# A third tile of the first head block as float32 products, other groups for the layer norm's factors, and x ahead of the weights in the opening of an attention and mixer-MLP kernel

## The chip, the cores and the metric

One Trainium2 chip, one core. The core has five engines that run their own queues and meet at semaphores: TensorE (PE; its weight loads are listed as PEld), VectorE (DVE), ScalarE (ACT), GpSimd (POOL) and SyncE (SP), from whose queue this kernel issues its DMA transfers. The metric is the time of one execution on the device in microseconds (us); lower is better. A kernel is executed several times, and the median stands for it.

## The reference

x has 2048 tokens of 512 channels. A layer norm without parameters is applied twice over, once for both branches and once more inside the second. Branch one is sliding-window attention with 32 heads of 16 channels, where each token sees itself and seven earlier ones at a distance of two. Branch two is an MLP 512 → 1376 → 512 with a tanh GELU.

```python
def _A_ref(x, wqkv, wo):                 # H=32 heads, Dh=16, W=8, dil=2
    qkv = (x @ wqkv).reshape(B, S, 3, H, Dh)      # -> q, k, v: B, H, S, Dh
    idx = pos[:, None] - (jnp.arange(W) * dil)[None, :]
    kg, vg = k[:, :, idx_c], v[:, :, idx_c]
    logits = einsum("bhsd,bhswd->bhsw", q, kg) * Dh ** -0.5   # idx < 0 masked
    o = einsum("bhsw,bhswd->bhsd", softmax(logits), vg)
    return o.reshape(B, S, D) @ wo
def _B_ref(x, w1, b1, w2, b2):
    h = gelu(layernorm(x) @ w1 + b1)
    return h @ w2 + b2
xn = layernorm(A_x)
return A_x + _A_ref(xn, wqkv, wo) * silu(_B_ref(xn, w1, b1, w2, b2))
```

## The kernel before, in words

Tokens are split into even and odd ones (`c` = 0, 1), since the window's distance is two; each half has eight tiles of 128 tokens by 512 channels, numbered 0 to 7. The heads come in four blocks of eight (`hb`). A unit is one half with one head block: its q, k, v columns (384) for eight tiles, then the attention of these heads on DVE and POOL. The MLP's two layers (`mlp1`, `mlp2`) run on TensorE between the units, so that DVE has time for the attention.

Products are made from f16 numbers in three passes: each operand is split into a high part (rounded to f16) and a low part (what is left), and high by high, low by high and high by low are summed. One tile's product with one head block is therefore 12 matmuls of 128x128 by 128x384. The weights are first scaled by a power of two that comes from their sum of squares (`scale_q`, L597 on ACT with `s` as its sum; L513 the sum over partitions on TensorE; L524 to L542 the exponent arithmetic on DVE, which yields `qsc`, `hsc`, `zsc`, `osc`). Then the high part is made on ACT (L619, L565) or DVE (L563), the low part on DVE (L626, L569) or, where a table says 'pool', by two POOL operations (L553 scales, L554 subtracts).

A planner records every operation with what it reads and writes, and issues them in the order of a table of operation numbers, `ORDER`; each engine works through its own part of that order. Which engine makes which part stands in tables at the top: `HI_ENG`, `W1ENG` (high parts), `QLO0`, `W1LO`, `W2LO` (low parts), `EV0`, `EV1` (which engine moves a finished product from its bank to SBUF). Buffers come from rings: `prod` (three of 128x2048, which also hold staged x and weights in the opening), `f`, and in PSUM `ps` (three banks), `pl` and `z0` to `z3` (one each). `U_93` and `U_94` are the two large SBUF buffers of the units' q, k, v; in the opening U_94 holds the transposed x and staged weights.

The opening belongs to the even half. Loads stand in SP's queue in the order of `LOADS`. Each tile of x (L1233) gets its statistics on DVE (L659, L660), then, for a group of tiles at once (`GROUPS`), `pb` on DVE (L714, L716) and the factor `rb` by a power on POOL (L718); `y` = normalised x is made on POOL (L748), ACT (L744) or DVE (L751), by tile. Tiles 0 to 3 are transposed on TensorE (L766: four transposes into a bank `z`), the high part is taken by ACT or DVE (L770, L772), the low part by DVE (L773). Tiles 4 to 7 get their f16 parts first (L756, L757) and are transposed by DMA (L758). The second norm's factor `cT` is made for a batch of tiles (`BATCHES`, L727 to L731) and folded into the scale with which a product leaves its bank (`cs`).

Those transposes and parts take time in which TensorE would have nothing to do. So for two tiles, 6 and 7 (`FP`), the product with the first head block is made directly in float32, from a transposed copy of x that the kernel loads ready-made (`A_xt`, L1258). `center(i)` takes the mean off: the sum over the four channel groups by DVE (L685) and one float32 matmul with a constant (L691), or the whole mean by four float32 matmuls (L682), as `MEANBY` says, then a subtraction in place on DVE (L693). `direct(i)` then makes four float32 matmuls 128x384 with the staged, unscaled weights (L700) into `pl` or a bank `z`. In the profile a float32 matmul shows as two rows. Later head blocks and the MLP use tiles 6 and 7 by the usual way.

TensorE's clock is kept up in the first microseconds by dummy matmuls (`WAKE`, L1305). After the opening come the units' matmuls (L864), evictions (L878 on DVE, L882 on ACT) and, from about 34 us, `mlp1` (L1143; its high part by ACT in L1156 and L1159, its low part by DVE in L1161) and `mlp2` (L1186, with the remainder in L1174 and L1177). The attention's multiplications and sums are L930, L933, L983 and L988 on DVE and L999 and L1010 on POOL. The output product is L1056 and L1088.

Of the kernel before, what the change touches and what calls it, by code (L numbers as in the profile page):

```python
# [10 lines left out]
BF16 = mybir.dt.bfloat16  # L11
# [7 lines left out]
P = 128  # L19
# [5 lines left out]
NI = 8  # L25
# [7 lines left out]
LASTP = 256  # L33
# [11 lines left out]
FP = (6, 7)  # L45
XC = (6, 7)
BYDMA = (4, 5, 6, 7)
TRZ = (3, 3, 0, 2, 0, 1, 1, 0)
PTR = (0.5487, 0.3388, 0.0342, 0.6565, 0.7826, 0.1978, 0.0549, 0.9)
GROUPS = ((0,), (1, 2), (3, 4, 5), (6, 7))  # L50
BATCHES = ((0, 1, 2, 3, 4, 5), (6, 7))
LOADS = (('t', 6), ('q', 0), ('q', 2), ('x', 2), ('x', 0), ('q', 4), ('t', 7), ('x', 5), ('x', 1), ('x', 3), ('x', 4), ('q', 6), ('w', 0), ('w', 2), ('x', 7), ('c', 2), ('s', 1), ('c', 0), ('w', 3), ('x', 6), ('w', 1), ('c', 1), ('b', 0), ('s', 0))
# [16 lines left out]
W2LATE = 6  # L69

# [309 lines left out]

# [1146 lines left out]
```

## Time and profile before

| what | value |
|---|---|
| median of 3 runs | 412.66 us (412.56 to 412.87) |
| span of the profiled execution | 411.0 us; its own time is not on the page |
| PE busy | 402.8 us (98%), 2030 matmul rows |
| DVE busy | 381.6 us (93%) |
| ACT busy | 224.9 us (55%) |
| POOL busy | 132.7 us (32%) |

The page and the answers of the trace share one manner of writing. `ps<-wq,yT` is an operation that reads buffers wq and yT and writes ps; `128x384 f32<-128x512 f32` are the shapes and types out and in; `x8` counts instructions of the same kind that follow each other; times are microseconds from the span's start. `<-DVE U L693` names what released an instruction after a wait: DVE's write of U in line 693. L numbers are lines of the kernel.

### The profile page before, as it was taken

What the parts mean: (1) busy time and instruction counts of PE and PEld (TensorE: products, weight loads), DVE (VectorE), ACT (ScalarE), POOL (GpSimd) and SP (SyncE); (2) the same over time, 40 slices, a digit from 0 to 9 for tenths busy, and PEclk for the clock granted to TensorE, in tenths of its full rate; (3) what the DMA queues carried; (4) which work ended last, traced back from release to release, by engine and by line L of the source; (5) the groups of instructions that cost most, each with busy time, mean ns of one, the idle gap of its engine ahead of it and who ended that gap; (6) DMA issues with size and microseconds to landing.
All of it is one profiled execution on the core that took longest, in us unless ns stands there. A gap on an engine that the chain in (4) does not pass through costs nothing.

```text
span 411.0 us, 5490 instructions
## 1 busy us (share of the span) xinstructions
PE 402.8 (98%) x2030; PEld 198.7 (48%) x2030; DVE 381.6 (93%) x386; ACT 224.9 (55%) x372; POOL 132.7 (32%) x141
## 2 busy tenths in 40 slices
PE   7899999999999999999999999999999999999996
PEld 4565544444444455445544554444445544444443
DVE  4899999999999999999889999899999989989985
ACT  3899987983989736633564164214523177236310
POOL 2843000053562425143424243233322505250012
PEclk9999999999999999999999999999999999999999
DMA  8957538251018372911251009610344452004984
GB/s 288 395 104 227 177 90 214 92 179 27 1 30 189 85 130 77 150 49 27 51 141 27 0 2 213 209 50 22 107 122 120 107 135 60 0 1 116 285 214 162
DMA packets 52627, 48.04 MB, mean 117 GB/s; under 512 B 37066, under 2 KB 37510, under 8 KB 52088
## 3 DMA queue, kind: packets, MB, share of 16 engines
q1 hardware_dynamic: 52600, 47.69, 42.8%
q8 instruction: 16, 0.26, 0.3%
q14 instruction: 11, 0.09, 0.1%
HBM read 24.40 MB, written 7.34 MB: 77 GB/s over the span
## 4 chain that ended last, share of the span: by engine, by line
PE 90%; DVE 3%; ACT 3%; DMA 1%; POOL 1%; issue 0%; SPq 0%; POOLq 0%; ACTq 0%; DVEq 0%
PE ps L864 27%; PE z L1186 25%; PE ps L1143 25%; PE ps L1056 5%; PE z L1088 2%; PE ps L1088 2%; PE z L1174 2%; DMA prod<-in_A_x_dram 1%; DVE bn L659 1%; ACT w L565 1%; ACT w L504 1%; PE pl L1088 1%; PE z L1177 1%; PE pl L864 1%; POOL prod L748 1%; DVE yT L773 0%
## 5 line engine op out<-in xcount | busy, mean ns | idle before, releaser
L864 PE MATMUL ps<-wq,yT 128*128 128x384 f16 (+1 forms) x708 | 128.9, 337 | 0.2
L1186 PE MATMUL z<-w,h 128*128 128x512 f16 x480 | 111.4, 379 | 0.0
L1143 PE MATMUL ps<-yT,w 128*128 128x512 f16 x480 | 109.0, 379 | 0.0
L864 PEld LDWEIGHTS <-yT 128*128 128x128 f16 x744 | 72.2, 98 | 59.1 <-issue 1.3
L930 DVE TENSOR_TENSOR prod<-U 128x2048 f32<-128x2048 f32 x32 | 73.8, 2312 | 4.1 <-ACT U L882 3.0
L1143 PEld LDWEIGHTS <-w 128*128 128x128 f16 x480 | 46.8, 98 | 55.6 <-issue 0.5
L933 DVE TENSOR_REDUCE L<-prod 128x128 f32<-128x2048 f32 x32 | 73.0, 2282 | 0.5
L1186 PEld LDWEIGHTS <-h 128*128 128x128 f16 x480 | 46.5, 98 | 54.6 <-issue 0.7
L999 POOL TENSOR_TENSOR prod<-prod,prod 128x1024 f32<-128x1024 f32 x14 | 41.3, 2968 | 81.3 <-DVE prod L988 81.3
L882 ACT ACTIVATE U<-ps,cs 128x384 f32<-128x384 f32 x54 | 30.1, 575 | 62.9 <-PE ps L864 62.7
L988 DVE TENSOR_TENSOR prod<-pl,U 128x2048 f32<-128x2048 f32 x28 | 63.5, 2283 | 0.3
L1156 ACT ACTIVATE ps<-ps,b1T,hsc 128x512 f32<-128x512 f32 x40 | 29.8, 747 | 37.0 <-PE ps L1143 36.8
L1159 ACT ACTIVATE h<-ps,hsc 128x512 f16<-128x512 f32 x40 | 27.4, 684 | 20.6 <-PE z L1186 19.7
L1009 POOL COPY gate<-prod 1x1 f32<-1x1 f32 x21 | 4.6, 219 | 102.2 <-DVE prod L930 102.2
L1010 POOL TENSOR_TENSOR prod<-prod 128x1024 f32<-128x1024 f32 x14 | 32.9, 2348 | 0.0
L1161 DVE SCALAR_TENSOR_TENSOR h<-ps,hsc,h 128x512 f16<-128x512 f32 x40 | 29.5, 744 | 3.2 <-ACT h L1159 3.2
L1056 PE MATMUL ps<-wo,oT 128*128 128x512 f16 x96 | 21.5, 379 | 0.0
L983 DVE TENSOR_TENSOR prod<-prod,prod 128x2048 f32<-128x2048 f32 x9 | 20.6, 2288 | 0.2
L971 ACT ACTIVATE o<-prod,osc 128x1024 f16<-128x1024 f32 (+1 forms) x9 | 9.5, 1051 | 18.0 <-DVE prod L983 9.9
L1010 POOL TENSOR_TENSOR prod<-prod,prod 128x1024 f32<-128x1024 f32 x7 | 16.4, 2347 | 0.0
L1088 PEld LDWEIGHTS <-oT 128*128 128x128 f16 x108 | 10.5, 98 | 10.4 <-issue 0.2
L1056 PEld LDWEIGHTS <-oT 128*128 128x128 f16 x96 | 9.4, 98 | 11.1
(201 smaller groups left out, 393.6 us busy)
## 6 DMA issues: line engine op xcount, KB each, us to landing
f<-in_A_x_dram SPq DMA_DIRECT2D x31, 256.0 KB, 3.1
U<-U SPq DMA_DIRECT2D x16, 392.0 KB, 6.7
gd<-f SPq DMA_DIRECT2D x12, 256.0 KB, 2.7
prod<-in_A_x_dram SPq DMA_DIRECT2D x8, 256.0 KB, 5.7
oT<-in_B_w_dram SPq DMA_DIRECT2D x2, 1024.0 KB
yT<-in_B_w_dram SPq DMA_DIRECT2D x2, 1024.0 KB
f<-gd SPq DMA_DIRECT2D x8, 256.0 KB, 5.4
out_dram<-f SPq DMA_DIRECT2D x8, 256.0 KB
```

The source lines that it names most:

```text
L864: nc.tensor.matmul(b.t[:, 0:wide], y[:, s, k, o:o + P], wq[hb][:, t, k], start=(n == 0), stop=(n == 11))
L882: act(384, lambda i=i, b=b: nc.scalar.activation(U3[:, i:i + 31:15, :], b.t[:, 0:384].rearrange("p (t e) -> p t e", t=3), AF.Identity, sca ...
L930: dve(2048, lambda p2=p2, g=g: nc.vector.tensor_tensor(p2(), q, slots(Ut, KH, 2 * g), op=ALU.mult), qk + [("kh", ub, 0), ("kh", ub, 1), (" ...
L933: dve(2048, lambda pr=pr, g=g: nc.vector.tensor_reduce(L3()[:, 2 * g:2 * g + 2], pr.t.rearrange("p (r f d) -> p r f d", r=2, d=DH), AX.X, ...
L988: dve(2048, lambda: nc.vector.tensor_tensor(pr.t.rearrange("p (r f d) -> p r f d", r=2, d=DH), A3()[:, 2 * g:2 * g + 2].rearrange("p r (f ...
L999: pool(2.4, lambda n=n: nc.gpsimd.tensor_tensor(acc.t[:, n:n + 1024], acc.t[:, n:n + 1024], p1.t[:, n:n + 1024], op=ALU.add), [acc, p1], [ ...
L1010: nc.gpsimd.tensor_tensor(x.t[:, 0:1024], x.t[:, 0:1024], y(), op=ALU.add)
L1056: nc.tensor.matmul(b.t, oT[:, hb, i // 4, s, i % 4], wo[:, t, hb], start=(hb == 0 and n == 0), stop=(hb == last and n == 2))
L1088: nc.tensor.matmul(b.t[:, cols], oT[:, hb, i // 4, s, i % 4], wo[:, t, hb, cols], start=(start and hb == 0 and n == 0), stop=(stop and hb ...
L1143: nc.tensor.matmul(b.t[0:M], w1[:, s, f * 512 + k * M:f * 512 + (k + 1) * M], yT[ch][:, t, k], start=(n == 0), stop=(n == 11))
L1156: act(512, lambda: nc.scalar.activation(b.t[0:M], b.t[0:M], AF.Gelu_apprx_tanh, bias=b1T[0:M, f:f + 1], scale=hsc[0:M, 1:2]), [b, ("b1T",) ...
L1186: nc.tensor.matmul(z.t, hl[s][:, t * P:(t + 1) * P], w2[:, w, f], start=(f == 0 and n == 0), stop=False)
```

## The change

It does the following.

- Tile 5 joins tiles 6 and 7: its product with the first head block is made in float32 into a third bank (z2). Its sum is taken by DVE. Its transposed x is a third load of that kind, and takes a place of its own in U_94.
- The groups of the layer norm's factor are (0), (1, 2), (3, 4), (5, 6, 7) instead of (0), (1, 2), (3, 4, 5), (6, 7), and the batches of the second factor (0 to 4), (5, 6, 7).
- SP's queue begins with x of tiles 0, 2 and 1, and the first half of the weights comes after x of tile 6 and two transposed tiles.
- 28 dummy matmuls instead of 19.
- Other engines for some parts: three of w1's high parts, and half of the second head block's, move from ACT to DVE; low parts of w1 move from DVE to POOL, and of w2 index 3 instead of index 5 is POOL's; of the evictions some change between ACT and DVE.
- A new table `ORDER`, and planner prices for POOL's operations. Several new options (`SUBS`, `ST_ENG`, `YLO`, `SECS`, `QH0`) stand at values that leave the code as it was; `LASTC` gives the same two parts as `LASTP` did.

```diff
-FP = (6, 7)
-XC = (6, 7)
+FP = (6, 7, 5)
+XC = (6, 7, 5)
-TRZ = (3, 3, 0, 2, 0, 1, 1, 0)
+TRZ = (3, 3, 3, 0, 0, 2, 0, 0)
-GROUPS = ((0,), (1, 2), (3, 4, 5), (6, 7))
-BATCHES = ((0, 1, 2, 3, 4, 5), (6, 7))
+GROUPS = ((0,), (1, 2), (3, 4), (5, 6, 7))
+BATCHES = ((0, 1, 2, 3, 4), (5, 6, 7))
-HI_ENG = ('act', 'act', 'act', 'dve', 'dve', 'dve', 'dve', 'act')
-XT = (0, 4, 30, 34)
+HI_ENG = ('act', 'act', 'act', 'act', 'act', 'dve', 'dve', 'act')
+XT = (0, 4, 30, 34, 8, 12)
-W1ENG = ('act', 'dve', 'act', 'act', 'act', 'act', 'act')
+W1ENG = ('dve', 'dve', 'dve', 'act', 'dve', 'act', 'act')
-W2LO = ('dve', 'dve', 'dve', 'dve', 'dve', 'pool', 'dve')
-EV0 = ('act', 'dve', 'dve', 'act', 'act', 'act', 'dve', 'dve')
-EV1 = ('dve', 'dve', 'act', 'act', 'act', 'act', 'dve', 'act')
-QLO0 = ('pool', 'dve', 'dve', 'pool')
+W2LO = ('dve', 'dve', 'dve', 'pool', 'dve', 'dve', 'dve')
+EV0 = ('act', 'dve', 'act', 'act', 'act', 'dve', 'act', 'act')
+EV1 = ('dve', 'dve', 'act', 'dve', 'act', 'act', 'act', 'act')
+QLO0 = ('dve', 'pool', 'pool', 'dve')
-W1LO = ('dve', 'dve', 'pool', 'dve', 'dve', 'dve', 'dve')
+W1LO = ('pool', 'dve', 'dve', 'pool', 'dve', 'pool', 'pool')
-MEANBY = ('dve', 'pe', 'pool', 'pool')
+MEANBY = ('dve', 'pe', 'dve', 'dve')
+QH1 = ('act', 'dve')
...
 ORDER = (
-    0, 1, 235, 19, 2, 3, 4, 5, 6, 7, 8, 9, 10, 11, 110, 111, 112, 113, 114, 115, 116, 117, 118, 119, 120, 121,
...
+    6, 118, 116, 117, 5, 119, 120, 121, 8, 122, 123, 124, 125, 45, 46, 0, 126, 61, 62, 20, 127, 17, 128, 129,
...
-WAKE = 19
+WAKE = 28
-IORD0 = (6, 7, 0, 4, 1, 3, 2, 5)
+IORD0 = (6, 7, 5, 0, 4, 1, 3, 2)
...
     def direct(i):
-        b = pb[i] = ([R_pl] + R_z[1:])[FP.index(i)].new()
+        b = pb[i] = ([R_pl] + R_z[1:] + R_z[:1] + [R_ps] * 3)[FP.index(i)].new()
...
     def on_pool(n, hi, src, s, r, w, **k):
-        pool(0.3 + n * POOL1, lambda: nc.gpsimd.tensor_scalar(hi, src(), s, 1.0, op0=ALU.mult, op1=ALU.mult),
-             r, [w], port=False, **k)
+        pool(0.121 + n * 1.1e-3, lambda: nc.gpsimd.tensor_scalar(hi, src(), s, 1.0, op0=ALU.mult, op1=ALU.mult),
+             r, [w], **k)
...
+            elif he == "dve":
+                dve(n, lambda src=src, dst=dst: nc.vector.tensor_scalar(
+                    dst[0], src(), qsc[:, hb, 0:1], None, op0=ALU.mult), r, hk, f=0.72, holds=stkey[hb])
```

Three places of the order are shown, as the instructions stand on their engines. Lines after the change are L1276 for loads of x, L1301 for the transposed x, L594 for the weights, L673 and L674 for the statistics, L705 for the sum, L717 for the subtraction, L714 and L702 for the two kinds of mean, L725 for the float32 product, L809 for the transposes, L559 and L560 for POOL's low parts.

SP's queue at the start, before: transposed x of tile 6, all of the first block's weights, x of tiles 2 and 0, and so on.

```order
L1258 DMA U_94<-in_A_xt_dram 128x512
L588 DMA prod_100<-in_A_wqkv_dram 128x768 x2
L1233 DMA prod_101<-in_A_x_dram 128x512 x2
L588 DMA U_94<-in_A_wqkv_dram 128x768
L1258 DMA U_94<-in_A_xt_dram 128x512
```

The same place after: x of tiles 0, 2, 1, then transposed 6, x of 6, transposed 7, the first half of the weights, x of 7, transposed 5, the second half.

```order
L1276 DMA prod_100<-in_A_x_dram 128x512 x3
L1301 DMA U_94<-in_A_xt_dram 128x512
L1276 DMA prod_101<-in_A_x_dram 128x512
L1301 DMA U_94<-in_A_xt_dram 128x512
L594 DMA prod_102<-in_A_wqkv_dram 128x768
L1276 DMA prod_101<-in_A_x_dram 128x512
L1301 DMA U_94<-in_A_xt_dram 128x512
L594 DMA prod_102<-in_A_wqkv_dram 128x768
```

The weights moved behind three tiles of x and two transposed tiles. On DVE the opening before starts with tile 6's sum and subtraction.

```order
L685 TENSOR_REDUCE f_103<-U_94 128x128
L693 TENSOR_TENSOR U_94<-U_94,ps_143 128x512
L659 BN_STATS bn_139<-prod_101 128x6
L660 BN_AGGR mv_153<-bn_139 128x2
L659 BN_STATS bn_140<-prod_101 128x6
```

DVE after starts with the statistics of three tiles.

```order
L673 BN_STATS bn_139<-prod_100 128x6
L674 BN_AGGR mv_153<-bn_139 128x2
L754 TENSOR_SCALAR pb_154<-mv_153 128x1
L673 BN_STATS bn_140<-prod_100 128x6
L674 BN_AGGR mv_153<-bn_140 128x2
L673 BN_STATS bn_141<-prod_100 128x6
L674 BN_AGGR mv_153<-bn_141 128x2
L705 TENSOR_REDUCE f_103<-U_94 128x128
L754 TENSOR_SCALAR pb_154<-mv_153 128x2
L673 BN_STATS bn_142<-prod_101 128x6
L674 BN_AGGR mv_153<-bn_142 128x2
L717 TENSOR_TENSOR U_94<-U_94,ps_143 128x512
```

The sum and the subtraction that TensorE's first product needs moved behind three statistics. TensorE before, from tile 6's product on:

```order
L700 MATMUL pl_146<-prod_100,U_94 128x384
L682 MATMUL ps_144<-U_94,first 128x128 x4
L700 MATMUL pl_146<-prod_100,U_94 128x384
L513 LDWEIGHTS fours
L513 MATMUL ps_145<-s_127,fours 128x1
L766 MATMUL z_150<-first,prod_101 128x128 x4
L700 MATMUL z_148<-prod_100,U_94 128x384 x4
L766 MATMUL z_150<-first,prod_101 128x128 x4
```

TensorE after, from the end of the dummy matmuls on (z_150 takes the transposes, pl_146, z_148 and z_149 the products of tiles 6, 7 and 5):

```order
L809 MATMUL z_150<-first,prod_100 128x128 x4
L714 MATMUL ps_143<-f_103,first 128x128
L702 MATMUL ps_144<-U_94,first 128x128 x4
L725 MATMUL pl_146<-prod_102,U_94 128x384 x2
L809 MATMUL z_150<-first,prod_100 128x128 x4
L725 MATMUL z_148<-prod_102,U_94 128x384
L725 MATMUL pl_146<-prod_102,U_94 128x384
L519 LDWEIGHTS fours
L519 MATMUL z_147<-s_125,fours 128x1
L714 MATMUL ps_145<-f_104,first 128x128
L725 MATMUL z_148<-prod_102,U_94 128x384 x2
```

Tile 0's transposes moved ahead of every product, and both means ahead of the first product. POOL after, between the layer norm's factors and the first attention unit, where before stood two pairs of 384 and one of 1024:

```order
L559 TENSOR_SCALAR oT<-oT,hsc 128x512
L560 TENSOR_TENSOR w_86<-oT,w_86 128x512
L559 TENSOR_SCALAR oT<-oT,hsc 128x1024
L560 TENSOR_TENSOR w_86<-oT,w_86 128x1024
L559 TENSOR_SCALAR h_113<-h_113,hsc 128x384
L560 TENSOR_TENSOR wq_84<-h_113,wq_84 128x4x96
L559 TENSOR_SCALAR yT_92<-yT_92,zsc 128x1024
L560 TENSOR_TENSOR w_87<-yT_92,w_87 128x1024
L559 TENSOR_SCALAR o_112<-o_112,hsc 128x1024
L560 TENSOR_TENSOR w_86<-o_112,w_86 128x1024
```

Low parts of w1 and w2 moved here from DVE's queue.

More of the change, by code (lines that the diff above doesn't have):

```diff
@@ L32 @@
 NFB = 7
-LASTP = 256
+LASTC = (0, 256, 512)
 LASTPOOL = (0, 2, 4)
@@ L363 @@
 PMEAN = 0.04
-PDIR = (0.192, 0.1517, 0.1187, 0.1556)
+PDIR = (0.192, 0.1517, 0.1187, 0.1556, 0.15, 0.15)
 PG = (0.5671, 0.5205, 0.3952, 0.4033)
@@ L618, in prep_q @@
             hk = [("wqh", hb, j) for j in range(k, k + st)]
-            act(n, lambda src=src, dst=dst: nc.scalar.activation(
-                dst[0], src(), AF.Identity, scale=qsc[:, hb, 0:1]), r, hk, holds=stkey[hb])
+            he = (QH0, QH1)[hb][k // st] if hb < 2 else "act"
+            if he == "pool":
+                pool(0.121 + n * 1.1e-3, lambda src=src, dst=dst: nc.gpsimd.tensor_scalar(
+                    dst[0], src(), qsc[:, hb, 0:1], 1.0, op0=ALU.mult, op1=ALU.mult), r, hk, holds=stkey[hb])
+            elif he == "dve":
+                dve(n, lambda src=src, dst=dst: nc.vector.tensor_scalar(
+                    dst[0], src(), qsc[:, hb, 0:1], None, op0=ALU.mult), r, hk, f=0.72, holds=stkey[hb])
+            else:
+                act(n, lambda src=src, dst=dst: nc.scalar.activation(
+                    dst[0], src(), AF.Identity, scale=qsc[:, hb, 0:1]), r, hk, holds=stkey[hb])
             lo = dict(r=r + hk, w=[("wq", hb, j) for j in range(k, k + st)], holds=stkey[hb], prio=PQLO if hb == 0 else None)
@@ L671, in tile_mixer, with parts, xcs @@
     xt = {i: U[1][:, XT[n] * P:(XT[n] + 4) * P].rearrange("p (k t) -> p k t", k=KT) for n, i in enumerate(FP)}
+    def parts(i):
+        return ((0, 1), (1, KT)) if i in SUBS else ((0, KT),)
+    def xcs(i):
+        return [("xc", i, k0) for k0, k1 in parts(i)]
     def center(i):
@@ L686, in center @@
                 [("xt", i)], [f], port=False, c=0.45)
+        elif MEANBY[n] == "add":
+            dve(256, lambda: nc.vector.tensor_tensor(f3(), x3[:, 0:2], x3[:, 2:4], op=ALU.add), [("xt", i)], [f])
+            dve(P, lambda: nc.vector.tensor_tensor(f3()[:, 0], f3()[:, 0], f3()[:, 1], op=ALU.add), [f], [f])
         else:
@@ L691, in center @@
             pe(1, P, lambda: nc.tensor.matmul(b.t[:, 0:P], mean1, f3()[:, 0], start=True, stop=True), [f], [b], fp32=6, prio=PMEAN)
-        m = lambda: b.t[:, 0:P].rearrange("p (o t) -> p o t", o=1).to_broadcast([P, KT, P])
-        dve(512, lambda: nc.vector.tensor_tensor(x3, x3, m(), op=ALU.subtract), [b, ("xt", i)], [("xc", i)], port=False, c=0.16)
+        for k0, k1 in parts(i):
+            m = lambda k0=k0, k1=k1: b.t[:, 0:P].rearrange("p (o t) -> p o t", o=1).to_broadcast([P, k1 - k0, P])
+            dve(P * (k1 - k0), lambda k0=k0, k1=k1, m=m: nc.vector.tensor_tensor(
+                x3[:, k0:k1], x3[:, k0:k1], m(), op=ALU.subtract), [b, ("xt", i)], [("xc", i, k0)], port=False, c=0.16)
     pb = {}
     def direct(i):
-        b = pb[i] = ([R_pl] + R_z[1:])[FP.index(i)].new()
+        b = pb[i] = ([R_pl] + R_z[1:] + R_z[:1] + [R_ps] * 3)[FP.index(i)].new()
         for k in range(KT):
@@ L701, in direct @@
                 b.t[:, 0:384], xt[i][:, k], stq[0]()[:, k * 384:(k + 1) * 384], start=(k == 0), stop=(k == KT - 1)),
-                [("xc" if i in XC else "xt", i), ("stq", 0, k)], [b], fp32=4.5, holds=stkey[0], after=pl.users([b]))
+                [("xc", i, max(k0 for k0, k1 in parts(i) if k0 <= k)), ("stq", 0, k)], [b], fp32=4.5, holds=stkey[0], after=pl.users([b]))
     mv0 = sb.tile([P, NI, 2], F32, name="mv0")
@@ L706, in tile_mixer, with stats_act @@
     gof = {i: g for g in GROUPS for i in g}
+    def stats_act(i):
+        q, (x, xkey) = cpos[i], xk[i]
+        sm = R_s.new()
+        o, dst = (i % 4) * P, yT[i // 4]
+        junk = dst[:, 0, :, o:o + P].bitcast(BF16)
+        act(512, lambda: nc.scalar.activation(x(), x(), AF.Identity, accum_out=sm.t[:, 0:1]), [xkey], [xkey, (sm, 0)], aps=2)
+        act(1, lambda: nc.scalar.activation(mv0[:, q, 0:1], sm.t[:, 0:1], AF.Identity, scale=1.0 / D), [(sm, 0)], [("mv0", i)])
+        act(1, lambda: nc.scalar.activation(sm.t[:, 1:2], sm.t[:, 0:1], AF.Identity, scale=-D ** -1.5), [(sm, 0)], [(sm, 1)])
+        act(512, lambda: nc.scalar.activation(
+            junk, x().rearrange("p (k t) -> p k t", k=KT), AF.Square, bias=sm.t[:, 1:2], scale=D ** -0.5,
+            accum_out=mv0[:, q, 1:2]), [xkey, (sm, 1), ("mv0", i)], [("mv0", i), ("yh", 0, i)], aps=3)
     def ln0(g):
@@ L710, in ln0 @@
         for i in g:
+            if ST_ENG[i] == "act":
+                stats_act(i)
+                continue
             with pl.fuse():
@@ L851, in qkv @@
         cp = lambda i: cpos[i] if c == 0 else i
-        raw = pl.users([("xc", j) for j in FP]) if u == 1 else set()
+        raw = pl.users([x for j in FP for x in xcs(j)]) if u == 1 else set()
         wide = 384 + FL * (hb == HLAST)
@@ L1090, in mm @@
             return go
-        parts = [(i, slice(0, D)) for i in range(NI - 1)] + [(NI - 1, slice(0, LASTP)), (NI - 1, slice(LASTP, D))]
+        parts = [(i, slice(0, D)) for i in range(NI - 1)] + [(NI - 1, slice(a, b)) for a, b in zip(LASTC, LASTC[1:])]
         banks = {}
@@ L1291, in tile_mixer @@
                     y0(i)
-    for n, g in enumerate(BATCHES):
+    for n, g in enumerate(SECS):
         with prio(PSEC[n]):
@@ L1344, in tile_mixer @@
         hrem[:, :, :, P - FL:P - FL + 2], halves[:, 8:16].rearrange("p (a b c) -> p a b c", a=2, b=2), hsc[:, 2:3], 2.0,
-        op0=ALU.mult, op1=ALU.mult), [("hsc2",)], [("hrem",)], port=False)
+        op0=ALU.mult, op1=ALU.mult), [("hsc2",)], [("hrem",)])
     for m, (f0, f1) in enumerate(W1P):
```

12 lines of the change are left out of this document (10 added, 2 removed), and 122 rows, old and new, of the table ORDER.

## The prediction

> **What bounds the kernel now.** I read the page first: how busy each engine is, and the chain of work that ended last.
>
> ```profile
> span 411.0 us, 5490 instructions
> PE 402.8 (98%) x2030; PEld 198.7 (48%) x2030; DVE 381.6 (93%) x386; ACT 224.9 (55%) x372; POOL 132.7 (32%) x141
> ...
> PE 90%; DVE 3%; ACT 3%; DMA 1%; POOL 1%; issue 0%; SPq 0%; POOLq 0%; ACTq 0%; DVEq 0%
> ```
>
> TensorE is busy for 98% of the span and carries 90% of the chain. Second, the span cut into stretches (length; busy time of PE, PEld, DVE, ACT, POOL; granted clock, DMA share, GB/s), to see where the other 2% lie:
>
> ```profile
> 18.73:60.00 41.27, 41.00 (x234) 22.31 (x232) 39.24 (x65) 38.54 (x70) 9.47 (x8) 1.00 0.55 153
> 60.00:380.00 320.00, 319.91 (x1595) 154.33 (x1594) 305.49 (x257) 170.35 (x279) 109.02 (x113) 1.00 0.36 89
> 380.00:411.00 31.00, 27.17 (x138) 12.95 (x136) 24.92 (x26) 5.26 (x7) 4.18 (x3) 1.00 0.73 220
> ```
>
> From 18.73 us to 380 us TensorE has next to no idle time (0.27 us, then 0.09 us), so whatever TensorE work is added or saved there comes out one for one at the end. The last stretch idles while outputs drain, and the change leaves it as it is. What can move lies ahead of 18.73 us. Third, the waits of TensorE, where the second and third columns are total and number:
>
> ```profile
> PE z L1305 <- DVE first L440: 1.2, 1, 1.2
> PE ps L682 <- DMA U<-in_A_xt_dram: 1.1, 1, 1.1
> PE z L766 <- POOL prod L748: 0.7, 1, 0.7
> PE z L766 <- DVE ssq L524: 0.4, 1, 0.4
> ```
>
> All of these stand in the opening. Fourth, the timeline of TensorE there (start, length, what, in brackets the idle time before it):
>
> ```profile
> 1.19 3.57 PE L1305 MATMUL z<-first,fours 128*128 128x256 bf16 x16 [1.19 <-DVE first L440]
> 4.64 0.79 PE L691 MATMUL ps<-f,first 128*128 128x128 f32 x2
> 5.23 0.72 PE L1305 MATMUL z<-first,fours 128*128 128x256 bf16 x3
> 6.21 1.56 PE L700 MATMUL pl<-prod,U 128*128 128x384 f32 x4 [0.27 <-DVE U L693]
> ...
> 10.12 1.16 PE L682 MATMUL ps<-U,first 128*128 128x128 f32 x8 [1.14 <-DMA U<-in_A_xt_dram]
> 11.11 0.81 PE L700 MATMUL pl<-prod,U 128*128 128x384 f32 x2
> ...
> 12.61 0.66 PE L766 MATMUL z<-first,prod 128*128 128x128 f32 x4 [0.69 <-POOL prod L748]
> 13.11 2.75 PE L700 MATMUL z<-prod,U 128*128 128x384 f32 x8
> 15.81 0.66 PE L766 MATMUL z<-first,prod 128*128 128x128 f32 x4
> ...
> 16.33 1.46 PE L864 MATMUL ps<-wq,yT 128*128 128x384 f16 x8
> 18.24 0.66 PE L766 MATMUL z<-first,prod 128*128 128x128 f32 x4 [0.45 <-DVE ssq L524]
> 18.73 5.84 PE L864 MATMUL ps<-wq,yT 128*128 128x384 f16 x32
> ...
> 24.84 3.41 PE L864 MATMUL ps<-wq,yT 128*128 128x384 f16 x20
> 28.09 2.11 PE L864 MATMUL pl<-wq,yT 128*128 128x384 f16 x12
> ```
>
> Lengths overlap by the pipeline, so I price by the distance of starts: one tile's float32 product 15.81 − 13.11 = 2.70 us, one tile's four transposes 13.11 − 12.61 = 0.50, a mean on TensorE 11.11 − 10.12 = 0.99, a mean from DVE's sum 5.23 − 4.64 = 0.59, and one f16 matmul (28.09 − 24.84)/20 = 0.1625. By 18.73 us TensorE has done two products (5.40), three tiles' transposes (1.50) and eight f16 matmuls (1.30), together 8.20 us. The other 10.53 us went to dummy matmuls, two means and waiting. The change is worth what it cuts from these 10.53 us, less the work that it adds.
>
> **The work it adds.** Tile 5's first-head-block product becomes float32: 2.70 in place of twelve f16 matmuls, 12 × 0.1625 = 1.95, so +0.75. A third mean comes with it, from DVE's sum. The one of that kind in the trace took 0.59 between dummy matmuls, and the other kind 0.99 for eight passes, or 0.25 for two. Between these ends I take 0.35, since no dummies surround the new one. TensorE's work grows by 1.10 us.
>
> **The opening, step by step.** What feeds TensorE there are these steps:
>
> ```profile
> 3.56 1.03 DVE L685 TENSOR_REDUCE f<-U 128x128 f32<-128x512 f32 x1 [2.05 <-DMA U<-in_A_xt_dram]
> 4.54 0.84 ACT L597 ACTIVATE wq<-prod 128x768 bf16<-128x768 f32 x1 [2.53 <-DMA prod<-in_A_wqkv_dram]
> 5.47 0.69 DVE L693 TENSOR_TENSOR U<-U,ps 128x512 f32<-128x512 f32 x1 [0.89 <-PE ps L691]
> 7.08 0.84 ACT L597 ACTIVATE wq<-prod 128x768 bf16<-128x768 f32 x1 [1.60 <-DMA prod<-in_A_wqkv_dram]
> 7.76 0.69 DVE L659 BATCH_NORM_STATS2 bn<-prod 128x6 f32<-128x512 f32 x1 [1.60 <-DMA prod<-in_A_x_dram]
> 8.59 0.66 DVE L659 BATCH_NORM_STATS2 bn<-prod 128x6 f32<-128x512 f32 x1
> 9.81 0.57 POOL L718 TENSOR_TENSOR rb<-pb,halves 128x1 f32<-128x1 f32 x1 [6.62 <-DVE ssq L524]
> 10.49 2.07 POOL L748 TENSOR_SCALAR prod<-prod,mv,rb 128x512 f32<-128x512 f32 x1
> ```
>
> Landings first, read off the waits. The first 256 KB land at 3.5. Between x of tile 2 (7.76) and the transposed x of tile 7 (10.12) come 256 + 384 + 256 KB in 2.36 us, 0.67 for 256 KB. But the second half of the weights, 384 KB, came 7.08 − 4.54 = 2.54 us after the first half, where the steady rate gives 1.01: the transfers lost 1.5 us there, and the trace doesn't show to what.
>
> *Tile 0.* Its x is now the first load, there at 3.5. Before, its statistics began at 8.59 and its transposes at 12.61, 4.02 later over POOL's factor and product. So the transposes start near 7.6. The 28 dummies, at (4.64 − 1.19)/16 = 0.216 each, run from 1.19 to 7.2 and are covered by that chain; the nine more cost nothing unless it gets shorter by 0.4.
>
> *Tiles 2 and 1, then tile 6.* DVE now takes three statistics ahead of tile 6's sum. If the 1.5 us are lost again at the same time of the run, tile 1's x lands at about 5.7 rather than 4.9. Statistics follow each other by 8.59 − 7.76 = 0.83, so they end at 5.7 + 2 × 0.83 = 7.4; tile 6's transposed x, the fourth load, is there by 7.1 if the stall spans both. The sum takes 1.03, to 8.4; the subtraction starts 0.88 after a sum's end (4.59 to 5.47), at 9.3, and ends at 10.0. The mean of tile 7, on TensorE, fits in that gap. TensorE's steady work thus begins at 10.0, with only tile 0's transposes (0.50) behind it, and the first half of the weights has landed: x of tile 6, transposed x of tile 7 and those weights are 256 + 256 + 384 KB, the 2.36 us of above, so 9.4.
>
> *From 10.0 on.* The order of after gives TensorE tile 6's first two products (1.35), then tile 1's transposes. Tile 1's factor and product follow the pair's statistics over POOL and ACT and are ready near 10.7, before 11.35. The second half of the weights lands near 11.7, and the first matmul that reads it stands at 12.5. Tile 5's subtraction should be done near 15.0 for a use at 15.7. These margins are 0.6 to 0.8 us each, estimates by the rows above.
>
> **The sum.** Other than products, transposes and f16 matmuls, the opening costs 10.0 − 0.50 = 9.50 after, against 10.53 before; with the third mean 9.85, so −0.68. The third product adds 0.75. Net +0.07. The 0.27 us that TensorE idles between 18.73 and 60 may go or stay: between 0 and −0.27. I take all of it, because ACT, the engine with the least slack there after DVE (38.54 of 41.27), hands work to DVE in that stretch. That gives −0.2, a time of 412.4 us against the median of 412.66. The profiled span is 411.0, so 1.6 us lie around it, and I count them unchanged.
>
> **Moves between engines.** Conversions move from ACT to DVE (three w1 parts, half of the second block's high part), low parts from DVE to POOL, evictions from DVE to ACT:
>
> ```profile
> L563 DVE TENSOR_SCALAR w<-oT,hsc 128x512 f16<-128x512 f32 x1 | 0.5, 486 | 0.0
> L569 DVE SCALAR_TENSOR_TENSOR w<-oT,hsc,w 128x1024 f16<-128x1024 f32 x2 | 2.5, 1276 | 0.0
> L878 DVE TENSOR_SCALAR U<-ps,cs 128x384 f32<-128x384 f32 x5 | 3.0, 609 | 0.4 <-PE ps L864 0.4
> ...
> 33.05 1.12 POOL L553 TENSOR_SCALAR oT<-oT,hsc 128x1024 f32<-128x1024 f32 x1 [6.88 <-ACT w L565]
> 34.26 2.13 POOL L554 TENSOR_TENSOR w<-oT,w 128x1024 f16<-128x1024 f32 x1
> 35.69 0.71 DVE L1334 SCALAR_TENSOR_TENSOR s<-s,s 128x1 f32<-128x1 f32 x1
> 36.44 0.15 DVE L1337 TENSOR_SCALAR s<-s 128x1 f32<-128x1 f32 x1
> ```
>
> DVE gains a sum (1.03), a subtraction (0.69), the high parts (six times 0.486 and a bit, about 3.0) and loses two 1024-wide low parts (2.55), one of 384 (about 0.6) and two evictions (1.22): within half a microsecond of zero. POOL gains about 8 us, two 1024-wide pairs (3.25 each) and smaller ones, nearly all between 22 and 65 us, where it was busy 9.47 of 41.27. I cost these moves at nothing; their cover is POOL's idle time, and DVE's 2.0 idle us of that stretch (41.27 − 39.24).
>
> The row at 35.69 speaks against moving low parts to POOL: a one-element operation with two inputs took 0.71 where its neighbour took 0.15, and it ended at 36.40, just as POOL's two-input operation ended at 36.39. It waited 0.56 us for POOL. The Trainium skill, "SBUF — State Buffer", section "SBUF: two separate sides", states this as a rule: a DVE operation with two SBUF inputs and a GpSimd operation that reads SBUF share a port pair, as an exclusive lock held for a whole instruction. The trace agrees in this one place; by that rule the moves aren't free, and the sum would be the slower rival's.
>
> **Rivals.**
> - *The loads don't lose 1.5 us, or lose it elsewhere* (faster). Tile 1's x lands at 4.9 and tile 6's transposed x at 5.5; the sum starts near 6.0, the subtraction ends near 8.6, and the first weights land near 8.0. Steady work begins between 8.6 and 9.5: −0.5 to −1.4 beside the −0.2, so 411.0 to 412.0, say 411.5. For it: small loads come first now. Against it: the loss may belong to the time of the run, not to the weights.
> - *DVE and POOL lock each other* (slower). If half of POOL's 8 new us stand in DVE's way, DVE falls 4 us behind. It has 2.0 us to give in that stretch; the 14.5 us that it idles later (305.49 of 320) come after TensorE has waited. The MLP's low parts, which DVE makes and TensorE reads, come late once the loss passes those 2.0 us; above that it goes to the end one for one: +1 to +2.5, say 414. For it: the row at 35.69, and DVE's 2.3 us operations of attention run beside the new POOL work. Against it: before has 9.47 us of POOL there at no visible cost but 0.56.
> - *The opening gains nothing at all*, because DVE at 93% sets the pace once TensorE starts earlier: TensorE waits for low parts what it won, 412.7, no change.
>
> **How the numbers follow.** A change under 0.2% (0.83 us) is about what a measurement of this kernel can't tell from none. Forecast 412.4, chance 0.37, its own range 411.9 to 413.0; no gain, 0.06; both are "same", 0.43 less a little that spills over to faster: 0.40. Faster rival 0.33, with the spill 0.36. Slower rival 0.24. The range runs from the low end of the faster one, 410.9, to 413.9, the middle of the slower one, and leaves out about 0.18.
>
> **What would show it.** Profile of after: dummies over by 7.2 and transposes of tile 0 at 7.6; tile 6's subtraction ending at 10.0 (8.6 in the faster case); then no TensorE wait over 0.3 until 60 us, the first matmul on the MLP's second layer at about 59. The slower rival would show DVE operations with two inputs stretched beside POOL's between 22 and 65, and TensorE waiting for the MLP's low parts after 55. I would be wrong if a feeder with a margin of 0.6 (tile 5's subtraction, the second half of the weights) came late by more, or if the order past 60 us made new waits.

## The result and the profile after

The changed kernel takes 423.88 us (median of 4 runs, 422.81 to 426.78) against 412.74 in the same series: a ratio of 1.0286, 95% interval 1.026 to 1.0313. It is slower by 11 us, where I had forecast no change and gave "slower" 0.24, at 414. In the experiments below, the executions profiled for e1 and h2 and one execution of e2 ran at a lower mean granted clock (0.66, 0.75 and 0.85, against 0.99 to 1.00 in the others) and are left out, so that e1 and h2 have times but no trace.

The page of the changed kernel, the same lines as of before:

```profile
span 422.5 us, 5529 instructions
PE 407.5 (96%) x2037; PEld 200.4 (47%) x2037; DVE 384.6 (91%) x386; ACT 226.3 (54%) x375; POOL 140.7 (33%) x147
...
DVE 37%; PE 34%; issue 10%; ACT 8%; DMA 7%; POOL 1%; SPq 1%; DVEq 0%; ACTq 0%
```

TensorE's share of the chain fell from 90% to 34%, and DVE's rose from 3% to 37%, though DVE is *less* busy than before (91%, was 93%). No engine has become the bound. The engines wait for each other. This execution took 424.31 us for its span of 422.5.

Where the waiting is, first in the timeline of TensorE in the opening:

```profile
1.19 5.57 PE L1348 MATMUL z<-first,fours 128*128 128x256 bf16 x28 [1.19 <-DVE first L446]
7.47 0.66 PE L809 MATMUL z<-first,prod 128*128 128x128 f32 x4 [0.72 <-POOL prod L788]
8.39 0.49 PE L714 MATMUL ps<-f,first 128*128 128x128 f32 x2 [0.26 <-DVE f L705]
...
9.85 1.56 PE L725 MATMUL pl<-prod,U 128*128 128x384 f32 x4
11.24 0.60 PE L809 MATMUL z<-first,prod 128*128 128x128 f32 x4
```

Tile 0's transposes start at 7.47 and the first product at 9.85, and no wait follows until 50 us. The opening is as forecast (7.6 and 10.0). Then the stretches from 30 us on, of before and, below it, of after (columns as in the prediction):

```profile
30.00:60.00 30.00, 29.87 (x166) 15.83 (x164) 28.49 (x40) 27.75 (x50) 3.25 (x2) 1.00 0.55 160
60.00:205.00 145.00, 144.91 (x727) 70.14 (x726) 139.42 (x133) 97.16 (x175) 52.13 (x55) 1.00 0.41 95
205.00:380.00 175.00, 175.00 (x870) 84.19 (x869) 166.07 (x125) 73.18 (x105) 56.89 (x58) 1.00 0.31 84
```

```profile
30.00:60.00 30.00, 28.53 (x158) 15.12 (x156) 23.01 (x37) 24.90 (x48) 9.14 (x7) 1.00 0.58 175
60.00:205.00 145.00, 143.75 (x714) 68.51 (x712) 140.29 (x129) 94.68 (x173) 52.37 (x55) 1.00 0.38 92
205.00:380.00 175.00, 169.66 (x839) 81.64 (x838) 160.84 (x116) 74.34 (x106) 58.98 (x60) 0.99 0.30 82
```

Before, TensorE idles 0.13, 0.09 and 0.00 us in them; after, 1.47, 1.25 and 5.34. Between 30 and 60 us DVE is busy 5.5 us less, in part since POOL now has its low parts (with most of them back on DVE, in e3 below, it is busy 2.1 us more), in part since what comes next on DVE isn't ready. Past 205 us, where the diff shows only new numbers in a table, lies the largest part. Where the loss begins is seen at the first matmul of the MLP's second layer, before which both kernels have done the same work (the changed one with twelve f16 matmuls fewer, for tile 5). The row of before, then that of after:

```profile
59.10 1.24 PE L1186 MATMUL z<-w,h 128*128 128x512 f16 x5
```

```profile
60.14 4.70 PE L1229 MATMUL z<-w,h 128*128 128x512 f16 x21
```

So 1.0 of the 11.5 us by which the span is longer are lost by then, and the rest behind. The waits of TensorE name many partners (us in total, times, longest):

```profile
PE ps L907 <- ACT U L925: 2.0, 1, 2.0
PE z L524 <- ACT w L510: 1.1, 1, 1.1
PE ps L907 <- DVE f L1113: 1.1, 1, 1.1
PE ps L1186 <- ACT first L929: 0.9, 1, 0.9
PE z L1217 <- DMA hl<-f: 0.8, 1, 0.8
...
PE z L1229 <- DVE h L1204: 0.7, 3, 0.3
```

One of them costs more than it shows (timeline of TensorE near 212 us, then the same place in the run e2 described below):

```profile
211.66 0.39 PE L1220 MATMUL z<-tail 34*128 34x512 f16 x2
214.07 3.79 PE L907 MATMUL ps<-wq,yT 128*128 128x384 f16 x12 [2.02 <-ACT U L925]
```

```profile
214.85 2.11 PE L907 MATMUL ps<-wq,yT 128*128 128x384 f16 x12 [2.01 <-ACT U L925]
```

The same twelve matmuls take 3.79 us in one trace and 2.11 in the other, behind the same wait. The granted clock is 0.50 from 214.3 to 217.6 us, and 1.00 at that place in e2: nine of the twelve stand 0.32 us apart instead of 0.16, so the wait cost another 1.7 us behind it. The Trainium skill, "TensorE: Matmul & The Clock Gate", section "What's actually happening", has the clock halved after an idle window of about 3.4 us that runs freely; here 2.0 us without a matmul sufficed in one of the two traces.

The traces account for nearly all of the loss. TensorE's idle time grows by 7.8 us from 30 to 380 us (8.06 against 0.22) and by 0.8 behind 380 us (4.64 against 3.83), and the slow matmuls add 1.7: together 10.3 of 11.5 us.

### The profile page after: what moved, and what is told of

It is laid out like the page before. It is cut to its first block, busy times and chain, and to the rows that moved or that the text cites. A ratio compares the mean times of both kernels' runs of the same rounds, so it can differ in the third digit from the quotient of the medians.

```text
span 422.5 us, 5529 instructions
## 1 busy us (share of the span) xinstructions
PE 407.5 (96%) x2037; PEld 200.4 (47%) x2037; DVE 384.6 (91%) x386; ACT 226.3 (54%) x375; POOL 140.7 (33%) x147
## 4 chain that ended last, share of the span: by engine, by line
DVE 37%; PE 34%; issue 10%; ACT 8%; DMA 7%; POOL 1%; SPq 1%; DVEq 0%; ACTq 0%
PE ps L907 10%; PE z L1229 10%; PE ps L1186 8%; DVE prod L973 8%; DVE L L976 8%; DVE prod L1031 5%; DVE h L1204 3%; DMA h<-in_B_w_dram 2%; DVE wq L640 2%; DVE prod L1026 2%; DMA yT<-in_B_w_dram 2%; PE ps L1131 2%; DMA U<-in_A_wqkv_dram 2%; PE z L1131 2%; PE ps L1099 1%
## 5 line engine op out<-in xcount | busy, mean ns | idle before, releaser
L1229 PE MATMUL z<-w,h 128*128 128x512 f16 x480 | 113.5, 379 | 0.7 <-DVE h L1204 0.7
L925 ACT ACTIVATE U<-ps,cs 128x384 f32<-128x384 f32 x55 | 31.0, 576 | 70.3 <-PE ps L907 54.9
L1042 POOL TENSOR_TENSOR prod<-prod,prod 128x1024 f32<-128x1024 f32 x14 | 38.0, 2734 | 90.3 <-DVE prod L1031 90.3
L1202 ACT ACTIVATE h<-ps,hsc 128x512 f16<-128x512 f32 x40 | 27.2, 683 | 14.5 <-PE z L1229 10.3
L999 ACT ACT_TABLE_LOAD x8 | 10.3, 1283 | 19.4 <-DVE L L997 18.2
L1053 POOL TENSOR_TENSOR prod<-prod,prod 128x1024 f32<-128x1024 f32 x7 | 16.4, 2346 | 0.0
L1131 PEld LDWEIGHTS <-oT 128*128 128x128 f16 x108 | 10.4, 98 | 11.3 <-DMA oT<-o 1.0
```

Source lines behind the costliest of these rows:

```text
L925: act(384, lambda i=i, b=b: nc.scalar.activation(U3[:, i:i + 31:15, :], b.t[:, 0:384].rearrange("p (t e) -> p t e", t=3), AF.Identity, sca ...
L1042: pool(2.4, lambda n=n: nc.gpsimd.tensor_tensor(acc.t[:, n:n + 1024], acc.t[:, n:n + 1024], p1.t[:, n:n + 1024], op=ALU.add), [acc, p1], [ ...
L1053: nc.gpsimd.tensor_tensor(x.t[:, 0:1024], x.t[:, 0:1024], y(), op=ALU.add)
L1229: nc.tensor.matmul(z.t, hl[s][:, t * P:(t + 1) * P], w2[:, w, f], start=(f == 0 and n == 0), stop=False)
```

## The experiments

All kernels are built from the changed source. Where an experiment mixes the two orders, every operation keeps its neighbours in the order that it is taken from. The first experiments weighed these theories: TAIL, the order past 58 us (the first matmul of the MLP's second layer) is what costs; DEBT, the stretch up to there leaves DVE behind; LOCK, POOL's new low parts and DVE block each other. Later ones add SPREAD: many places of the order cost one or two us each.

**e1 and g1: changed head, earlier order behind.**

```diff
 ORDER: operations that stood ahead of the first mlp2 matmul: as changed
-ORDER: the others as changed
+ORDER: the others as in the kernel before
```

> The changed kernel with its loads, tables and order up to the first matmul of the MLP's second layer (about 58 us), and from there on the instructions in the order of the kernel before. Theory TAIL (the new order of everything past 58 us is what costs 11 us): 412 to 413.5 us. Theory DEBT (the changed stretch up to 58 us leaves DVE behind, and DVE never makes it up): 419 to 424 us, as the changed kernel. Theory LOCK (low parts moved to POOL stretch DVE's operations): 418 to 424 us, since the engine tables are those of the changed kernel.

> The changed kernel's loads, tables and order up to about 58 us with the earlier order behind, once more, for an undisturbed trace: 417 to 419 us. Theory SPREAD (each place where two engines' orders no longer meet costs TensorE one to two us; the changed order past 58 us has most of them, the joint of the two orders the rest): TensorE's waits lie between 27 and 100 us, close to the joint, and none behind 140 us. Rival DEBT (DVE is behind from 58 us on and stays so): TensorE's waits go on to the end.

417.76 us, ratio 1.0118 (1.0093 to 1.0143), and again 417.48, 1.013 (1.0113 to 1.0147). Six of the eleven us go with the order behind 58 us; the time lies between the ranges of e1. The trace is g1's. TensorE idles in it 2.5 us from 30 to 60 and 2.9 from 60 to 205, and not at all past 205:

```profile
30.00:60.00 30.00, 27.47 (x152) 14.60 (x151) 22.35 (x34) 23.83 (x47) 13.59 (x8) 1.00 0.48 147
60.00:205.00 145.00, 142.11 (x705) 67.89 (x704) 143.54 (x133) 95.88 (x172) 53.15 (x55) 1.00 0.40 98
205.00:380.00 175.00, 175.00 (x875) 84.71 (x873) 164.29 (x124) 74.61 (x109) 58.98 (x59) 1.00 0.29 78
```

This is against DEBT as a cause of the late waits: DVE stands idle for 7.65 us from 30 to 60 here too, and past 100 us nothing of it is left. TensorE's waits from 30 us on lie between 50 and 99 us, as SPREAD had it.

**e2: earlier head, changed order behind.**

```diff
 ORDER, tables, loads up to the first mlp2 matmul: as in the kernel before
+ORDER: the others as changed
```

> The kernel before with its loads, tables and order up to the first matmul of the MLP's second layer, and from there on the instructions in the order of the changed kernel. TAIL: 420 to 424 us. DEBT and LOCK: 412 to 414 us.

423.8 us, 1.0259 (1.0229 to 1.0289), as TAIL forecast. The order past 58 us alone, with no third tile, no moved load in the opening and no low part on another engine, costs 11 us:

```profile
60.00:205.00 145.00, 141.27 (x701) 67.40 (x700) 140.29 (x129) 91.94 (x167) 46.13 (x52) 1.00 0.37 88
205.00:380.00 175.00, 169.78 (x847) 81.80 (x845) 162.14 (x119) 75.35 (x107) 58.98 (x60) 1.00 0.31 82
```

Its largest waits of TensorE past 58 us are those of the changed kernel, in the same lines, but the one at 72 us for a low part of DVE is longer (1.8 us for 0.6), and one at 124 us for an eviction is new:

```profile
PE ps L907 <- ACT U L925: 2.0, 1, 2.0
PE ps L1186 <- DVE h L1204: 1.8, 1, 1.8
PE ps L907 <- DVE f L1113: 1.1, 1, 1.1
PE ps L1186 <- ACT U L925: 1.0, 1, 1.0
```

The two halves don't add: the changed head costs 5 us with the earlier order behind it, the changed order 11 us behind the earlier head, and both together 11 us. A mixture has waits that neither kernel has, so these runs put the share of the changed order past 58 us between 6 and 11 us.

**e3 and e4: the low parts of w1 and w2 on the other kernel's engines.**

```diff
 # e3, in the changed kernel; e4 is the reverse, in the kernel before
-W2LO = ('dve', 'dve', 'dve', 'pool', 'dve', 'dve', 'dve')
+W2LO = ('dve', 'dve', 'dve', 'dve', 'dve', 'pool', 'dve')
-W1LO = ('pool', 'dve', 'dve', 'pool', 'dve', 'pool', 'pool')
+W1LO = ('dve', 'dve', 'pool', 'dve', 'dve', 'dve', 'dve')
```

> The changed kernel with the low parts of w1 and w2 on the engines of the kernel before (DVE for four of w1 and one of w2 that POOL now makes, POOL for one of each), all else as changed, the order too. LOCK: 413 to 417 us. TAIL: 421 to 425 us. DEBT: 420 to 424 us, or a little less if the debt comes from POOL's late parts.

> The kernel before with the low parts of w1 and w2 on the engines of the changed kernel, all else as before. LOCK: 416 to 420 us. TAIL: 412.5 to 414 us. DEBT: between, 413 to 416 us, if late low parts make it.

e3: 426.0 us, 1.0334 (1.0291 to 1.0376), above all three ranges and no better than the changed kernel. With the low parts back, TensorE's idle time falls from 1.5 to 0.4 us between 30 and 60 and grows from 1.3 to 4.7 between 60 and 205. So the moved low parts aren't the cause of its loss, as LOCK would have it, in the order that was made for them. e4: 419.97, 1.0178 (1.0153 to 1.0203), as LOCK forecast, but by a single wait and with POOL as the one that is held up most. First TensorE's, then POOL's, then DVE's rows:

```profile
54.09 4.45 PE L1186 MATMUL ps<-yT,w 128*128 128x512 f16 x10 [4.86 <-POOL w L560]
```

```profile
43.92 4.04 POOL L560 TENSOR_TENSOR w<-o,w 128x1024 f16<-128x1024 f32 x1
47.95 4.85 POOL L559 TENSOR_SCALAR oT<-oT,hsc 128x512 f32<-128x512 f32 x1
52.88 1.16 POOL L560 TENSOR_TENSOR w<-oT,w 128x512 f16<-128x512 f32 x1
```

```profile
43.38 8.93 DVE L973 TENSOR_TENSOR prod<-U 128x2048 f32<-128x2048 f32 x3
```

POOL's scaling of 512 columns takes 4.85 us beside DVE's three attention multiplications, where it took 1.06 in the changed kernel, and TensorE waits 4.86 us for the part; ten matmuls behind the wait take 4.45 us, about twice their usual time, at a granted clock of 0.50 (54 to 58 us). DVE's three took less before than the 8.93 us here:

```profile
43.42 6.68 DVE L930 TENSOR_TENSOR prod<-U 128x2048 f32<-128x2048 f32 x3
```

The lock of the prediction exists, and in the order of before it costs 7 us, wait and slow matmuls together. The changed order has POOL make this part at 34.18 us, ahead of DVE's first attention multiplication (44.42), and so avoids this wait.

**f1, f2 and h2: the cover of the exponential**, which is work that DVE does while ACT makes it. DVE's longest waits in the changed kernel look like a cause:

```profile
DVE mx L1001 <- ACT L L999: 8.6, 6, 2.0
DVE h L1204 <- ACT h L1202: 8.5, 5, 2.5
```

Before, the first of them is 1.0 us: between the subtraction and the sum over the exponentials stands another operation of 1.3 us or more. The order rows of one of five edited places (f1 against the changed kernel):

```diff
 L997 TENSOR_TENSOR L_111<-L_111,mx_116 128x512
+L1016 SCALAR_TENSOR_TENSOR o_112<-prod_102,osc,o_112 128x2x512
 L1001 TENSOR_REDUCE mx_117<-L_111 128x64
 L1002 RECIPROCAL mx_117<-mx_117 128x64
...
 L1204 SCALAR_TENSOR_TENSOR h_114<-ps_144,hsc,h_114 128x512
-L1016 SCALAR_TENSOR_TENSOR o_112<-prod_102,osc,o_112 128x2x512
```

> The changed kernel, but in five of the eight softmaxes ACT makes the high part of the previous unit's attention output ahead of the exponential, and DVE its low part (1.28 us) between the subtraction and the sum that needs the exponential, as the kernel before has it. Theory COVER (past 58 us DVE stands idle behind ACT's table load and exponential, 8.6 us in six places, and TensorE then waits for DVE): 4 to 6 us less than the changed kernel, 418 to 420 us. Rival HEAD (the stretch up to 58 us sets the loss, DVE's later idle time is only its sign): 422 to 425 us.

> The kernel before with the reverse edit: in five softmaxes the output's high part follows the exponential on ACT and its low part follows the first multiplication by v on DVE, so that DVE waits for the exponential with little beside it. COVER: five times 1.0 to 1.3 us of DVE, some of it hidden in DVE's slack: 415 to 418 us. HEAD: 412 to 413.5 us.

f1: 423.33 us, 1.028 (1.0247 to 1.0313), no change, as HEAD had it. The wait at 212 us shrank from 2.0 to 0.2 us and DVE's waits for the exponential from 8.6 to 3.1, but TensorE waits 2.1 us at 349 instead, and there too the clock falls to 0.50 behind the wait (twelve matmuls of 512 columns take 4.44 us instead of 2.75). f2, the reverse edit in the kernel before: 417.65, 1.0136 (1.0121 to 1.0151), which looks like COVER, but the trace says otherwise. DVE waits 6.0 us for the exponential there, and TensorE waits nowhere new from 60 to 380 us, save 0.3. Nor is DVE behind: it begins the last softmax's sum at 374.32 us, and at 374.13 before. The time is lost at the end. The edit has DVE make the low part of the seventh unit's output at 378.63 us instead of 372.01, and its transfer and those behind it in SP's queue start more than 6 us later:

```profile
384.37 0.82 PE L1131 MATMUL ps<-wo,oT 128*128 128x512 f16 x3 [2.06 <-DMA oT<-o]
398.87 0.82 PE L1131 MATMUL pl<-wo,oT 128*128 128x512 f16 x3 [2.03 <-DMA oT<-o]
```

So the idle time of DVE behind the exponential doesn't by itself make the loss in either kernel. The edit was tried once more, on top of the moved load of g4:

> The changed kernel with both edits: w2's load ahead (421.5 us by itself) and the cover of the exponential (423.3 by itself, 0.5 less than the changed kernel). If the 2.4 us at 212 and the slower clock behind it go through once nothing earlier is late: 417.5 to 419.5 us. If DVE's order past 260 us takes it back, as in the run with the cover alone: 420.5 to 422 us.

422.86 us, 1.0261 (1.0244 to 1.0278), against 1.0227 without the cover: worse, and above both ranges.

**f3 and f4: only the opening, or the order up to 58 us, with the engines of before.**

```diff
-W1ENG = ('dve', 'dve', 'dve', 'act', 'dve', 'act', 'act')
+W1ENG = ('act', 'dve', 'act', 'act', 'act', 'act', 'act')
 # EV0, EV1, W1LO, W2LO and QH1 as before too; ORDER past 27 us (f3) or 58 us (f4) as before
```

> Only the opening of the change: third float32 tile, groups, loads, dummy matmuls and the order up to about 27 us, with the engines for weights and evictions and everything later in order as before. The prediction's sum for the opening, which the changed profile agrees with up to 27 us (steady work from 10 us on): 412.0 to 412.9 us. If the opening itself leaves engines behind (HEAD): 415 us or more.

> As the run with the changed kernel's head and the earlier order from 58 us on, which took 417.8 us, but with w1's and w2's parts, the second block's high part and the evictions on the engines of the kernel before. If its 5 us come from POOL's low parts (late, and locking DVE): 412.5 to 414 us. If they come from the order between 27 and 58 us: 416 to 418 us.

f3: 421.76 us, 1.0224 (1.0205 to 1.0244), far above the prediction's sum, so that the alternative held; f4: 419.71, 1.0181 (1.0166 to 1.0196), above both ranges. The waits of f3 lie between 21 and 52 us, 7.4 us in eight places, led by

```profile
PE ps L907 <- DVE wq L640: 2.5, 2, 2.1
PE pl L907 <- ACT U L925: 2.2, 2, 1.5
PE pl L907 <- ACT f L796: 1.1, 1, 1.1
```

The longest, at 31 us, is for a low part of the first block's weights. They are loaded later in the changed opening, and DVE makes this part at 30.66 us, about when the changed kernel does (30.39); the kernel before has all four by 20.5 us, and its order asks for it 2.1 us too soon here. The opening is not a part that can be had by itself: its price is what follows.

**g2, g3: which half of the changed order.** Both in the kernel before.

```diff
 ORDER up to 58 us: as before
+ORDER: 58 to 205 us as changed, then as before         # g2
+ORDER: as before to 205 us, then as changed            # g3
```

> The kernel before up to 58 us, the changed order from 58 to about 205 us (the fourth softmax), the earlier order behind. With the changed order from 58 us to the end it took 423.8. SPREAD: the waits of the trace between 58 and 205 us are 5.0 us of some 10, so 417 to 419.5 us. If it is one place in the second half: 412 to 414.5 us; if one in the first half: 422 to 424 us.

> The kernel before up to the fourth softmax at about 205 us, the changed order behind. SPREAD: 2.4 us at 212 with the slower clock after it and 5 us in smaller waits: 416.5 to 419.5 us. One place in the first half: 412 to 414 us.

g2: 415.67 us, 1.0088 (1.0072 to 1.0105). g3: 416.84, 1.0109 (1.0092 to 1.0126). Each half costs; the sum, 3.6 + 4.8 = 8.4 us, falls short of e2's 11.2, and the wait at 212 us, 2.0 us in e2, is in neither of the two; the orders meet close to it. SPREAD held in g3, while g2 came out 1.3 us below its range, and above that of a single place in the second half. Past 205 us TensorE idles 3.3 us in g3, 0.00 in g2.

**g4, h3, h1: the load of w2.** In the changed kernel TensorE waits 1.1 us at 52 us for ACT's sum over w2. ACT waits for the load, which SP issues at 42.18, behind the halo transfers (`U<-U`, `v<-U`).

```diff
 SP's queue in the changed order:
+load of w2 (yT), two small loads of w2
 U<-U, U<-U, v<-U
-load of w2 (yT), two small loads of w2
```

> The changed kernel with the second large load of w2 and two small ones ahead of the halo transfers in SP's queue, where they stood behind them. TensorE waits 1.1 and 0.3 us at 52 us for the sum over w2 that hangs on this load. If that wait goes through to the end: 422 to 423 us. If DVE has the say from there on: 423.5 to 424.5 us, no change.

> The changed kernel with w2's load ahead up to the fourth softmax at about 205 us, the earlier order behind. Past 205 us TensorE waits 9.0 us in all there with the clock's 1.5 us, against 2.6 us in the same places before: 414.5 to 416.5 us if these waits are the rest. If DVE is behind from the first half: 418 us or more.

> The changed loads, tables and order up to 58 us with w2's second large load ahead of the halo transfers, and the earlier order from 58 us on. Without the load's move it took 417.5 us, with waits of TensorE of 2.8 us at 50 to 53 (that load) and 2.7 us at 72 to 75. If the head loses by the load alone: 413 to 415 us. If the waits at 72 to 75 are a matter of DVE being behind from 30 to 58 us: 415.5 to 417 us.

g4: 421.49 us, 1.0227 (1.0212 to 1.0243); the wait is gone and 2.4 us with it, 0.5 us below its first range. h3, with the earlier order past 205 us besides: 415.01, 1.0063 (1.0042 to 1.0084), within its first range. The waits past 205 us are worth 6.5 us, and in its trace they are gone:

```profile
60.00:205.00 145.00, 143.73 (x714) 68.42 (x713) 140.28 (x129) 93.76 (x171) 51.78 (x55) 1.00 0.38 93
205.00:380.00 175.00, 175.00 (x876) 84.93 (x875) 167.11 (x128) 75.80 (x109) 59.23 (x60) 1.00 0.31 82
```

h1, the moved load in the kernel of e1: 417.78, 1.0132 (1.0115 to 1.0149), nothing gained, and above both ranges. The wait for w2 went, but a wait for a low part of DVE came, 1.4 us at 57, and that of 2.2 us at 75 in g1 stayed (2.1). The load is a cause in the one order and not in the other.

**j1: the third tile alone, in the kernel before.** Tile 5's product leaves its bank with the scale of the f16 products here, so that block's values for it are off; no operation is left out.

```diff
-FP = (6, 7)
+FP = (6, 7, 5)
 # ('t', 5) loaded behind ('t', 7); its operations put into ORDER by hand
```

> The kernel before with tile 5 as a third float32 product and nothing else of the change: its transposed x is loaded behind tile 7's, its sum and subtraction follow tile 0's low part on DVE, its mean and its four products go into TensorE's order behind the first eight f16 matmuls, and tile 5's twelve f16 matmuls of the first block are gone. TensorE's work grows by the 1.1 us of the prediction's sum, less up to 0.6 us of waiting that it may fill: 412.5 to 413.2 us. If DVE's 1.7 us more in the opening make its later work late, as the tables of this kernel leave little room: 414 to 417 us.

415.2 us, 1.007 (1.0042 to 1.0098): 2.9 us slower, within the second range. In the traces the span grows by 2.4 us: TensorE is busy 0.65 us longer (403.44 against 402.79, where the sum had 1.1), and a wait of 1.7 us for an eviction at 44 us, which the kernel before doesn't have, is the rest:

```profile
PE ps L907 <- ACT U L925: 1.7, 1, 1.7
```

## Why the prediction was wrong

*The opening held.* Dummies under cover, transposes of tile 0 at 7.47 (7.6 forecast), statistics at 5.70 and 6.53 (5.7 and 6.5), first product at 9.85 (10.0), no wait from there to 50 us. At the first matmul of the MLP's first layer TensorE was 0.3 us ahead (34.29 us with four f16 matmuls more done, tile 5's left out, against 33.97). The statistics that waited for the second and third load began at 5.7, as forecast, so the faster rival's condition (4.9) wasn't met in this trace:

```profile
5.70 0.69 DVE L673 BATCH_NORM_STATS2 bn<-prod 128x6 f32<-128x512 f32 x1 [1.19 <-DMA prod<-in_A_x_dram]
6.53 0.66 DVE L673 BATCH_NORM_STATS2 bn<-prod 128x6 f32<-128x512 f32 x1
```

*The step that failed* stands in the first part: "whatever TensorE work is added or saved there comes out one for one at the end". It took TensorE's 0.27 and 0.09 us of idle time past 18.73 us for a property of the kernel. It is a property of the one order. DVE is busy 95% of 60 to 380 us and TensorE 100%, both in order, and they hand work to each other some forty times over ACT. The order of before makes every one of these meetings; the changed one, a new table from end to end, misses some. I had read that table at three places of the opening, and listed "if the order past 60 us made new waits" among what would prove me wrong without giving it a price or a chance. By the runs it gives between 6 us (e1, the changed kernel without it) and 11.2 us (e2, the kernel before with it).

*The sum by runs.* From 423.9: 2.4 us for w2's load in SP's queue (g4), 6.5 for the order past 205 us (h3), and 2.3 to 3.0 left (the kernel before took 412.74 us in the first series and 412.03 in h3's). In h3's trace TensorE idles 0.9 us between 30 and 60 us and 1.3 between 60 and 205, against 0.1 and 0.1 before. The third tile's work lies in the rest, which the runs don't part from what the opening gains.

*The moves between engines at nothing.* The cover that I named, POOL's idle time and DVE's 2.0 us, was there in the changed order: e3 gains nothing by undoing the low parts. It hangs on the order, though: in the earlier one the same moves cost 7 us (e4). And DVE, relieved, didn't get ahead; it idled 7.0 us from 30 to 60.

*The slower rival* had the right sign by the wrong mechanism. Lock rows are there: POOL's moved part of w2 takes 3.29 and 2.98 us at 59.7, where the same pair of operations takes 1.11 and 2.13 at 66. One of DVE's low parts of 768 columns takes 3.11 us at 134, the others 1.01, but e2 has that row too, beside POOL's work for the attention and not beside a moved part. e4 shows what the lock can do. By e3 it doesn't make the changed kernel's loss. *The faster rival* is not refuted as a price, only not met.

What stays open is why single waits past 205 us arise where they do. f1 removed one of them and another came, which speaks for the order as a whole, and I haven't found a smaller cause in it. No kernel of this study beats the one before.

## What to carry to other kernels

Where two engines are both above 90% and each runs in order, a trace without waits is evidence for its order, not for the slack of the kernel; a change that rewrites the order must be read to its end, stretch by stretch, before anything is booked "one for one". A list of an engine's longest waits is no list of causes: DVE's waits for the exponential cost TensorE next to nothing up to 380 us when 6.0 us of them stood in the kernel before, and taking 5.5 us of them away gained nothing; only swapping parts of the order between the two kernels told which stretch paid. A part of a change that sets when data land (here the loads) can't be judged without the order that was made for it.

## What the runs showed of the hardware

POOL can be held up for two DVE operations in a row: a scaling that took 1.06 us in the changed kernel took 4.85 in e4 beside two-input multiplications of DVE, and a two-input operation 4.04 instead of 2.13.

TensorE's granted clock fell to 0.50 behind five of the eleven places where the traces show TensorE waiting 2.0 to 2.2 us after the opening: at 214 us in the changed kernel, 211 in g4, 352 in f1, 33 in f3 and 76 in h1, each time for about 3.4 us. Behind the other six (one each in e2 and e3, two each in f2 and g1) it stayed at 1.00. Behind the one longer wait, 4.86 us in e4, it fell too. The twelve matmuls behind such a wait took 3.79 us (changed kernel) and 3.73 (g4), and 2.11 in e2.
